# A fused attention and MoE kernel: the last chunk's second layer in seven block products instead of eight

## The chip, the cores and the metric

The kernel runs on one core of one Trainium2 chip. The metric is the device time of one execution in microseconds (us). Five engines work side by side, each on its own queue of instructions in a fixed order: PE (TensorE, matrix products into PSUM), DVE (VectorE), ACT (ScalarE), POOL (GpSimd) and SP (SyncE, which here issues the DMAs). PEld is TensorE's loading of weights, which overlaps its products.

## The reference

```
attn_out = softmax(q k^T / 8 + decay, causal) v      # 8 batches, 8 heads, 576 positions, 64 per head
x = attn_out as 4608 tokens x 512
h = x @ w_in                                         # 512 x 2048
g = h * tanh(softplus(h))                            # Mish
out = g @ w_out                                      # 2048 x 512
```

All arrays are float32.

## The kernel before, in words

Attention runs over 32 pairs of heads (8 batches of 4 pairs). The MoE part works on 9 chunks of 512 tokens: chunks 0 to 7 are the first 512 positions of the eight batches, chunk 8 (the last) gathers the 64 last positions of each of them. A float32 matrix is held as two float16 parts, hi and lo, and a product is made of three TensorE products (hi hi, hi lo, lo hi). The 2048 hidden columns are 16 blocks of 128 (`NF`).

**First layer.** For one block `j` and one chunk, `m1_items` issues 4 x 3 = 12 products of 128 x 512 into one PSUM bank, ScalarE applies Mish (tile `me`), and `halves` scales and splits the result into `gh` and `gl`. In the chunks 7 and 8 the blocks are taken in pairs (`TWINS`), and `m1_seven` makes a pair's 2 x 2 block product by seven products of half the width instead of eight (the scheme of Strassen and Winograd): 7 x 2 x 3 = 42 products of 128 x 256 in place of 24 of 128 x 512. It needs sums of the tokens' blocks (`sums_of`) and sums of the weights' blocks (`diffs_of`), made by VectorE and ScalarE, and VectorE combines the seven results (`tt` on PSUM and an SBUF tile). Seven pairs are so done; the blocks 12 and 15 stay single.

**Second layer.** `m2_items` issues 4 x 3 products of 128 x 512 for one block into the four PSUM banks 4 to 7, which collect all 16 blocks of a chunk; then ScalarE copies each bank to `ot` and a DMA of 256 KB stores it. The first layer has the banks 0 to 3. In chunks 7 and 8 four blocks of the first layer and four of the second take turns (`GJ`).

**What sets the order.** The kernel's code records operations, it does not issue them. `Program` lists them with what they read and write, and a planner (`forward`, `backward`, `schedule`) simulates the five queues with costs of its own, ten times over, and writes out the order that came out best; where an operation may run on ScalarE or VectorE (`nc.choose`), it picks one. So an edit in the last chunk can move instructions anywhere in the program. All recorded operations carry the source line of one helper (L332 before, L335 now), so the groups of the trace are told apart by their tiles. `me` is a ring of five tiles (`NME`), `wall` holds all weights, `xa` the chunks' tokens.

Of the kernel before, what the change touches and what calls it, by code (L numbers as in the profile page):

```python
# [682 lines left out]
def attn_moe(ctx: ExitStack, tc: tile.TileContext, qk, v, f, w_in, w_out, out):  # L683
# [222 lines left out]
    def scale_weights(t0, t1):  # L906

        m, c, t, v = (a[:, t0:t1].rearrange("p t x -> p (t x)") for a in (wsq, wsc, wiv, wba))
        nc.vector.tensor_scalar(out=c, in0=m, scalar1=2.0**-120, scalar2=None, op0=ALU.max)
        twins = [a for a, b in TWINS if t0 <= a and b < t1]  # L910
        if twins:
            a, b = twins[0], twins[-1] + 2
            one, two = (wsq[:, a + k : b : 2, 0].unsqueeze(2).to_broadcast([P, len(twins), 2]) for k in range(2))
            nc.vector.scalar_tensor_tensor(
                out=wsc[:, a:b, 0].rearrange("p (t k) -> p t k", k=2), in0=one, scalar=2.0**-120, in1=two,
                op0=ALU.max, op1=ALU.add)
# [43 lines left out]

    def gated(c, js):
        nc.vector.scalar_tensor_tensor(
            out=gsc[c][:, js], in0=wsc[:, js, 0], scalar=csx[c], in1=fac[min(c, 1)][:, js],
            op0=ALU.mult, op1=ALU.mult)

    def level_all():
# [3 lines left out]
        level2(1, slice(0, NF), r)  # L970

    def split_weights(i):
        x, j = worder[i]
# [54 lines left out]
    def scale_chunk3(c, i):  # L1028
        cosc[c] = col()
        nc.vector.scalar_tensor_tensor(  # L1030
            out=cosc[c], in0=cix[c], scalar=1.0 / GSH, in1=top[:, i : i + 1], op0=ALU.mult, op1=ALU.mult)


    st = {g: {} for g in range(B * NP)}
# [109 lines left out]

    more_e = cp.tile([P, NEX, CH], F32, name="more_e")
    late = cp.tile([P, 704], F32, name="late")
    def mm(o, l, r, start, stop):
        nc.tensor.matmul(out=o, lhsT=l, rhs=r, start=start, stop=stop)

# [447 lines left out]
    def flat16(t):  # L1597
        return (t if len(t.shape) == 2 else t.rearrange("p j t s -> p (j t s)")).bitcast(F16)

    def sums_of(c):  # L1600
        t = xa[c % 2] if c < B else xat
        if c < B:
            halves = [flat16(xa[1 - c % 2])[:, 2048 * d : 2048 * d + 2048] for d in range(2)]
            homes = [(x[:, 0:1024], x[:, 1024:2048]) for x in halves]
        else:
            v = sp.tiles["v32"]
            homes = [[v[2 * d + k].bitcast(F16)[:, 0:1024] for k in range(2)] for d in range(2)]
        spare = [x[:, 0:CH] for x in sp.tiles["pt"] + sp.tiles["x32"]]
        for d in range(2):
            ga, gb, f1, f2 = spare[4 * d : 4 * d + 4]  # L1610
            hi, lo = homes[d]
            sums[c, d] = [x.rearrange("p (k n) -> p k n", k=4) for x in (hi, lo)]
            for g, dt in ((ga, d), (gb, d + 2)):
                nc.choose(*([(e, "tensor_tensor", (), dict(out=g, in0=t[:, dt, 0], in1=t[:, dt, 1], op=ALU.add))]
                    for e in ("vector", "gpsimd")))
            n1, n2 = slice(0, 256), slice(256, CH)
            tt = nc.vector.tensor_tensor
            tt(out=f1[:, n1], in0=ga[:, n2], in1=ga[:, n1], op=ALU.subtract)
            tt(out=f1[:, n2], in0=gb[:, n2], in1=ga[:, n2], op=ALU.subtract)
            tt(out=f2[:, n1], in0=f1[:, n2], in1=ga[:, n1], op=ALU.add)  # L1620
            tt(out=f2[:, n2], in0=gb[:, n1], in1=f2[:, n1], op=ALU.subtract)
            split(hi, lo, (f1, f2))

    def split(hi, lo, fs):
        for k, f in enumerate(fs):
            w = slice(CH * k, CH * k + CH)
            nc.choose(*(scaled(hi[:, w], f, None, e) for e in ("scalar", "vector")))
            nc.choose(*(sub(lo[:, w], f, hi[:, w], e) for e in ("vector", "gpsimd")))

    def diffs_of(a):  # L1630
        k = [x for x, _ in TWINS].index(a)
        home = flat16((sp.tiles["qk32"] + sp.tiles["hl"] + ST2 + ST1 + [rk2])[k])
        hi, lo = home[:, 0:1024], home[:, 1024:2048]
        w1, w2 = (wall[:, place[0, j]] for j in (a, twin_of[a]))
        fa, fb = (more_e[:, k] for k in range(2))
        s1, s2 = (x[:, 0:CH] for x in sp.tiles["v32"][4:6])
# [10 lines left out]
        split(hi, lo, (s1, s2))  # L1647

    nseven = [0]

    def m1_seven(c, a):
        j = twin_of[a]

        def both():
# [27 lines left out]
            p1 = sp.tiles["hb"][k % 2][:, n1]  # L1682
            tt = nc.vector.tensor_tensor

            def mish(o, i_, i):
# [23 lines left out]
    def m2_items(c, j):  # L1709
        n = min(CH, NT - c * CH)  # L1710

        def dts(k):
            gh, gl = gt[c, j]
            nc.closing = nc.closing or len(nc.ops)

            ends = [b - 1 for a, b in groups] if c == 0 else [NF - 1]
            if j in ends and k == 0:
                scale_chunk3(c, NG_ if c else ends.index(j))
            for dt in range(k * MQ, (k + 1) * MQ):
# [148 lines left out]
    def w0(fn):  # L1868
        M.append((fn, 0))
# [3 lines left out]
    for c in range(NCHUNK):  # L1873
        cstart[c] = len(M)
        if c == 1:
            w0(level_all)
        if c:
            w0(lambda c=c: scale_chunk2(c))
        if c == B:
            for b in range(B):  # L1880
                w0(lambda b=b: scale_tails(b))
        if c == 0:
            done = i = 0
            while done < NF:
                if i < NF:
                    M.extend(m1_items(c, i))
                n = 0
                while i - done >= LAG0 and n < 2 and done < NF:
                    M.extend(m2_items(c, done))
                    done += 1  # L1890
                    n += 1
                    if i - done < LAG:
                        break
                i += 1
            continue
        pairs_of = [a for a, _ in TWINS if c >= C7 and (a >= PLAIN or c > C7)]
        later = {b for a, b in TWINS if a in pairs_of}
        if pairs_of:
            w0(lambda c=c: sums_of(c))
        for j0 in range(0, NF, GJ):  # L1900
            phases += 1
            if c == C7:
                for a in pairs_of:
                    if j0 <= a < j0 + GJ:
                        w0(lambda a=a: diffs_of(a))
            if c == C7 + 1:
                for a, _ in TWINS:
                    if j0 <= a < j0 + GJ and a not in done7:
# [4 lines left out]
            phases += 1  # L1913
            for j in range(j0, j0 + GJ):
                M.extend(x + (phases,) for x in m2_items(c, j))
        if c == C7:
            done7 = pairs_of

    ai = 0

    def run_a(upto):
# [104 lines left out]
```

## Time and profile before

| | |
|---|---|
| median of 3 runs | 1014.02 us (1012.45 to 1014.3) |
| the profiled execution, its own time | 1017.58 us |
| its span on the engines | 1015.8 us |
| PE busy | 975.0 us, 96% of the span |
| DVE busy | 731.1 us, 72% |
| ACT busy | 710.1 us, 70% |
| POOL busy | 19.3 us, 2% |

The span runs from the first instruction to the last write; what the own time has beyond it (1.8 us) is start and end. A busy share is a mean over stages with different limits, so a stage is read by itself, and the chain of waits says which engine ended a stage.

### The profile page before, as it was taken

The numbers are of one execution on the slowest core, as the hardware profiler recorded it, in microseconds if no ns is written. First come the engines' busy times: TensorE is split into PE (matmuls) and PEld (weight loads), VectorE is DVE, ScalarE is ACT, GpSimd is POOL, SyncE is SP. The second block draws the span as 40 slices with busy tenths as digits, with TensorE's granted clock in tenths as the row PEclk, the third lists the DMA queues.
The fourth block names the chain that finished last, engine by engine and source line by source line (L and its number), as shares of the span: only waits on it lengthen the run. The fifth ranks groups of instructions, "written<-read, shape, count | busy, mean of one in ns | idle before, by whom it ended". The sixth has DMA issues, their size and how long they took to land.

```text
span 1015.8 us, 20884 instructions
## 1 busy us (share of the span) xinstructions
PE 975.0 (96%) x7847; PEld 545.8 (54%) x7847; DVE 731.1 (72%) x2013; ACT 710.1 (70%) x1369; POOL 19.3 (2%) x80
## 2 busy tenths in 40 slices
PE   6899699989999999999999999999999999999998
PEld 5686344544555455555555554454554556656664
DVE  7999799997677676667677667676666669953432
ACT  3569799987777877777778777888787765434323
POOL 5000000000000000000000000000000000000000
PEclk8899899999999999999999999999999999999999
DMA  7878967588777766676667686776566542001001
GB/s 209 335 251 210 182 159 157 115 178 192 137 143 163 168 136 147 147 176 138 151 145 184 144 158 139 178 136 134 127 111 143 92 74 63 4 1 42 1 1 42
DMA packets 265079, 137.50 MB, mean 135 GB/s; under 512 B 237522, under 2 KB 237714, under 8 KB 264978
## 3 DMA queue, kind: packets, MB, share of 16 engines
q1 hardware_dynamic: 264978, 136.17, 59.3%
q8 instruction: 61, 1.00, 0.4%
q14 instruction: 40, 0.33, 0.1%
HBM read 45.46 MB, written 9.66 MB: 54 GB/s over the span
## 4 chain that ended last, share of the span: by engine, by line
PE 66%; DVE 16%; ACT 7%; DMA 6%; issue 3%; SPq 1%; POOL 0%; DVEq 0%; ACTq 0%
PE b L332 66%; DVE wall L332 3%; DVE b L332 2%; DMA pt<-hb 2%; DVE hb L332 2%; DMA qk<-in_qk_dram 1%; ACT junk L332 1%; DMA st<-hl 1%; ACT L332 1%; DVE xp L332 1%; ACT hb L332 1%; DVE vv L332 1%; DVE x L332 1%; DVE gl L332 1%; ACT more_e L332 1%
## 5 line engine op out<-in xcount | busy, mean ns | idle before, releaser
L332 PEld LDWEIGHTS <-wall 128*128 128x128 f16 x3372 | 323.1, 98 | 345.7 <-issue 12.1
L332 PE MATMUL b<-gh,wall 128*128 128x512 f16 x1152 | 367.1, 379 | 1.5 <-DVE gh L332 1.5
L332 PE MATMUL b<-xa,wall 128*128 128x512 f16 (+1 forms) x1602 | 345.5, 365 | 6.2 <-ACT me L332 2.2
L332 PE MATMUL b<-gl,wall 128*128 128x512 f16 x576 | 218.1, 379 | 0.4 <-DVE gl L332 0.4
L332 DVE SCALAR_TENSOR_TENSOR gl<-me,gsc,gh 128x512 f16<-128x512 f32 x144 | 106.5, 746 | 52.0 <-ACT gh L332 51.0
L332 ACT ACTIVATE me<-b,cinv 128x512 f32<-128x512 f32 (+1 forms) x130 | 85.0, 660 | 53.1 <-PE b L332 52.2
L332 PE MATMUL b<-st 67*64 67x64 f16 (+11 forms) x672 | 105.3, 299 | 7.6 <-DVE x L332 3.0
L332 DVE CUSTOM_DVE_ANT_0 b<-b,mskw 128x512 f32<-128x512 f32 (+2 forms) x168 | 94.2, 563 | 21.1 <-PE b L332 19.8
L332 PE MATMUL b<-vv,pt 128*128 128x65 f16 (+3 forms) x2464 | 96.0, 199 | 7.3 <-DMA pt<-hb 6.0
L332 PEld LDWEIGHTS <-st 67*128 67x128 f16 (+3 forms) x864 | 67.7, 101 | 54.6 <-issue 13.1
L332 PEld LDWEIGHTS <-pt 128*128 128x128 f16 (+1 forms) x2352 | 78.4, 103 | 32.2 <-DMA pt<-hb 8.4
L332 ACT ACT_TABLE_LOAD x70 | 89.8, 1283 | 2.7 <-DVE x L332 1.5
L332 ACT ACTIVATE rk<-b,mn 128x512 f32<-128x512 f32 (+3 forms) x126 | 63.8, 541 | 39.7 <-DVE mn L332 32.7
L332 ACT ACTIVATE more_e<-b,mn 128x512 f32<-128x512 f32 (+3 forms) x126 | 64.0, 542 | 32.6 <-DVE mn L332 29.3
L332 DVE TENSOR_TENSOR hb<-rk,hb 128x512 f16<-128x512 f32 x84 | 57.7, 686 | 26.2 <-ACT hb L332 26.0
L332 DVE TENSOR_TENSOR hb<-more_e,hb 128x512 f16<-128x512 f32 x84 | 57.7, 687 | 24.7 <-ACT hb L332 24.3
L332 ACT ACTIVATE gh<-me,gsc 128x512 f16<-128x512 f32 x82 | 59.0, 720 | 2.5 <-DVE gsc L332 0.5
L332 ACT ACTIVATE hb<-more_e 128x512 f16<-128x512 f32 x84 | 52.6, 627 | 5.9 <-DMA pt<-hb 5.3
L332 ACT ACTIVATE hb<-rk 128x512 f16<-128x512 f32 x84 | 52.6, 627 | 3.0 <-DMA pt<-hb 2.5
L332 DVE TENSOR_SCALAR gh<-me,gsc 128x512 f16<-128x512 f32 x62 | 29.8, 483 | 31.8 <-ACT me L332 30.6
L332 DVE TENSOR_TENSOR me<-b,hb 128x256 f32<-128x256 f32 x42 | 17.4, 420 | 48.7 <-PE b L332 48.2
L332 DVE SCALAR_TENSOR_TENSOR hl<-qk,qt,hl 128x576 f16<-128x576 f32 x56 | 44.2, 811 | 0.5 <-DMA st<-hl 0.5
(187 smaller groups left out, 1048.8 us busy)
## 6 DMA issues: line engine op xcount, KB each, us to landing
st<-hl SPq DMA_DIRECT2D x168, 144.0 KB
qk<-in_qk_dram SPq DMA_DIRECT2D x30, 576.0 KB
out_dram<-ot SPq DMA_DIRECT2D x36, 256.0 KB
v<-in_v_dram SPq DMA_DIRECT2D x30, 288.0 KB
wall<-in_w_in_dram SPq DMA_DIRECT2D x16, 512.0 KB
wall<-in_w_out_dram SPq DMA_DIRECT2D x16, 512.0 KB
pt<-hb SPq DMA_TRANSPOSE x168
vv<-in_v_dram SPq DMA_DIRECT2D x2, 288.0 KB
```

What stands on the lines that cost most here:

```text
L332: r = getattr(real[eng], method)(*a, **kw)
```

## The change

The last chunk's second layer is made by seven block products as well. A pair of blocks of the hidden layer (two blocks of 128) meets the output's four blocks of 128: the 512 x 256 part of `w_out` and the pair's 256 x 512 activations make two such 2 x 2 block products (the index `e`), of seven products each, each of three 128 x 256 products on TensorE. So a pair costs 42 products of 128 x 256 in place of 24 of 128 x 512. `diffs2_of` makes the sums of blocks of `w_out` (once for each pair); `operands`, called at the end of `m1_seven` in the last chunk, makes the sums of the activations' blocks and splits four operands in place of the two of `halves`; `m2_seven` issues the products for a group of four pairs (`KG`), step after step, and VectorE or ScalarE adds each step's result to accumulators in SBUF (`accs`, in the tiles `xp0`, `hb` and `ot`), which eight DMAs of 128 KB store. All 16 blocks now form pairs, so blocks 12 and 15 go into pairs in the first layer of chunks 7 and 8 too. `scale_weights` no longer gives a pair one common scale; `ratio` corrects for it in `operands`. The preparation moves: `sums_of` and `scale_tails` of the last chunk into chunk 7, `diffs_of` of one pair into chunk 6, one `diffs_of` and one `diffs2_of` into chunk 4 (with `me` tiles as scratch), seven `diffs2_of` into chunk 7.

```diff
-TWINS = [(0, 1), (2, 3), (4, 5), (6, 7), (8, 9), (10, 11), (13, 14)]
+TWINS = [(2 * i, 2 * i + 1) for i in range(NF // 2)]
+C2 = 7
+KG = (4,4,)
+CE = 4
...
+    def diffs2_of(k):
...
+        fa, fb, s1, s2 = scratch(n == 0)
+        for i, f in enumerate((fa, fb)):
+            w = wall[:, place[1, 2 * k + i]]
+            nc.choose(*([(e, "tensor_tensor", (), dict(out=f, in0=w[:, 0:512], in1=w[:, 512:1024], op=ALU.add))]
+                for e in ("vector", "gpsimd")))
+        n1, n2 = slice(0, 256), slice(256, CH)
+        tt = nc.vector.tensor_tensor
+        tt(out=s1[:, n1], in0=fa[:, n2], in1=fb[:, n2], op=ALU.add)
+        tt(out=s1[:, n2], in0=s1[:, n1], in1=fa[:, n1], op=ALU.subtract)
+        tt(out=s2[:, n1], in0=fa[:, n1], in1=fa[:, n2], op=ALU.subtract)
+        tt(out=s2[:, n2], in0=fb[:, n1], in1=s1[:, n2], op=ALU.subtract)
+        split(hi, lo, (s1, s2))
...
+    def operands(c, a, u1, u2):
...
+        nc.vector.tensor_tensor(out=t12[:, n1], in0=u1[:, n2], in1=u1[:, n1], op=ALU.subtract)
+
+        def less(o, x, y):
+            nc.vector.scalar_tensor_tensor(out=o, in0=x, scalar=r, in1=y, op0=ALU.mult, op1=ALU.subtract)
+
+        less(t34[:, n1], u2[:, n2], u1[:, n2])
+        less(t12[:, n2], u2[:, n2], t12[:, n1])
+        less(t34[:, n2], u2[:, n1], t12[:, n2])
...
+        for (hi, lo), x, s in zip(res, (u1[:, n1], t12, t34, u2), (f, f, f, fj)):
...
+            nc.choose(*(scaled(hi, x, s, e) for e in GHW))
+            nc.choose(*(scaled_rest(lo, x, s, hi, e) for e in GLW))
+        ops2[c, k] = res
+
+    def m2_seven(c, ks, first, last):
...
+        def step(w, begins, a, b, to):
+            for e in range(2):
+                o = bank_of(e, w)
+                for n, k in enumerate(ks):
+                    for m, (h, l) in enumerate(((0, 0), (0, 1), (1, 0))):
+                        nc.tensor.matmul(
+                            out=o, lhsT=a(k, e, h), rhs=b(k, l), start=begins and n + m == 0,
+                            stop=n == len(ks) - 1 and m == 2, skip_group_check=not begins)
+                for q in to:
+                    x = accs[c][2 * (e + q // 2 * 2) + q % 2]
+                    if (e, q) not in done and first:
+                        done.add((e, q))
+                        nc.choose(*(scaled(x, o, cosc[c], g) for g in ("scalar", "vector")))
+                    else:
+                        nc.vector.scalar_tensor_tensor(
+                            out=x, in0=o, scalar=cosc[c], in1=x, op0=ALU.mult, op1=ALU.add)
...
+        steps = [
+            (0, True, weight(0, 0), value(0, None), (1, 2, 3)),
+            (1, True, diff(1), value(1, 1), (1,)),
+            (0, False, weight(1, 0), value(3, 0), (0,)),
+            (2, True, diff(0), value(1, 0), (3,)),
+            (1, False, diff(2), value(2, 0), (3,)),
+            (1, False, weight(1, 1), value(2, 1), (2,)),
+            (2, False, diff(3), value(3, 1), (1,))]
...
+            if c > C7:
+                operands(c, a, u1, u2)
+                return
             for i, u in ((a, u1), (j, u2)):
                 halves(c, i, u, CH)
...
         if c == B:
-            for b in range(B):
-                w0(lambda b=b: scale_tails(b))
+            for a, _ in TWINS:
+                M.extend(m1_seven(c, a))
+            k = 0
+            for i, n in enumerate(KG):
+                M.extend(m2_seven(c, range(k, k + n), i == 0, i == len(KG) - 1))
+                k += n
+            continue
...
+        def ahead_of_last(j0):
+            if j0 == 0:
+                w0(lambda: scale_chunk2(B))
+                for b in range(B):
+                    w0(lambda b=b: scale_tails(b))
+                w0(lambda: sums_of(B))
+            for k in ((5, 6, 7), (), (), range(4))[j0 // GJ]:
+                w0(lambda k=k: diffs2_of(k))
+        if c == C7 - 1:
+            w0(lambda: diffs_of(NF - 4))
+        if c == CE:
+            w0(lambda: diffs_of(NF - 2))
+            w0(lambda: diffs2_of(4))
```

Three places of the written order. First, VectorE's queue at the end of the last chunk's first layer. Before, it ends with the last pair's combinations (into `me` from a bank `b`) and the `lo` parts `gl`:

```order
L332 TENSOR_TENSOR me_1_162<-b0_0_125,hb_1_153 128x256
L332 SCALAR_TENSOR_TENSOR gl_0_161<-me_0_159,gsc3_102,gh_0_160 128x512
L332 TENSOR_TENSOR me_2_165<-b0_0_125,hb_1_153 128x256
L332 TENSOR_TENSOR me_2_165<-b1_0_118,me_2_165 128x256
L332 TENSOR_TENSOR me_2_165<-b0_0_125,hb_1_153 128x256
L332 TENSOR_TENSOR me_1_162<-b1_0_118,me_1_162 128x256
L332 TENSOR_SCALAR gh_2_166<-me_2_165,gsc3_102 128x512
L332 SCALAR_TENSOR_TENSOR gl_2_167<-me_2_165,gsc3_102,gh_2_166 128x512
L332 SCALAR_TENSOR_TENSOR gl_1_164<-me_1_162,gsc3_102,gh_1_163 128x512
```

Now, for a pair in the middle of that chunk, the same queue holds the operands' sums (in `more_e`, with `late` as the column `ratio`), four `lo` parts (in `wall` and `qk32`), and an accumulation from bank 4 into `ot`, between the combinations of the next pairs:

```order
L335 SCALAR_TENSOR_TENSOR more_e_104<-me_1_162,late_105,more_e_104 128x256
L335 TENSOR_TENSOR me_3_171<-b3_0_121,hb_0_152 128x256
L335 SCALAR_TENSOR_TENSOR wall_69<-me_0_159,gsc3_102,wall_69 128x256
L335 TENSOR_TENSOR me_3_171<-b0_0_125,me_3_171 128x256
L335 SCALAR_TENSOR_TENSOR more_e_104<-me_1_162,late_105,more_e_104 128x256
L335 TENSOR_TENSOR me_4_174<-b2_0_120,hb_0_152 128x256
L335 SCALAR_TENSOR_TENSOR wall_69<-more_e_104,gsc3_102,wall_69 128x2x256
L335 SCALAR_TENSOR_TENSOR qk32_0_108<-me_1_162,gsc3_102,qk32_0_108 128x512
L335 TENSOR_TENSOR me_3_171<-b3_0_121,hb_0_152 128x256
L335 SCALAR_TENSOR_TENSOR wall_69<-more_e_104,gsc3_102,wall_69 128x2x256
L335 SCALAR_TENSOR_TENSOR ot_0_191<-b4_0_122,cols_93,ot_0_191 128x256
```

What a pair asks of VectorE has more than doubled, and combinations, on which TensorE's banks 0 to 3 wait, stand behind it in one queue.

Second, TensorE's queue where the last chunk's first layer ends. Before, the last single block's products (bank 3) are followed by the last group of the second layer, in products of 512:

```order
L332 MATMUL b3_0_121<-xa2_91,wall_69 128x512
L332 LDWEIGHTS wall_69
L332 MATMUL b4_0_122<-gh_0_160,wall_69 128x512
L332 LDWEIGHTS wall_69
L332 MATMUL b5_0_123<-gh_0_160,wall_69 128x512
L332 LDWEIGHTS wall_69
L332 MATMUL b5_0_123<-gl_0_161,wall_69 128x512
```

Now the last pair's last product (bank 3) is followed by the second layer's first group in products of 256 (the weights' sums stand in `xa`):

```order
L335 MATMUL b3_0_121<-xa2_91,wall_69 128x256
L335 LDWEIGHTS late_105
L335 MATMUL b3_0_121<-xa2_91,late_105 128x256
L335 LDWEIGHTS xa1_90
L335 MATMUL b7_0_107<-gh_1_163,xa1_90 128x256
L335 LDWEIGHTS xa1_90
L335 MATMUL b7_0_107<-gl_1_164,xa1_90 128x256
```

At this point 117 of the second layer's 336 products are already issued, spread between the pairs of the first layer; 219 follow.

Third, VectorE's queue at the start of chunk 7, ahead of and around that chunk's first two combinations. Before, weights' sums stand there (tiles `v32`, `more_e`):

```order
L332 TENSOR_TENSOR me_3_171<-b1_0_118,hb_0_152 128x256
L332 TENSOR_TENSOR me_0_159<-b0_0_125,hb_1_153 128x256
L332 TENSOR_TENSOR me_3_171<-b2_0_120,me_3_171 128x256
L332 TENSOR_TENSOR more_e_104<-wall_69 128x512
L332 TENSOR_TENSOR me_3_171<-b1_0_118,hb_0_152 128x256
L332 TENSOR_TENSOR v32_4_137<-more_e_104 128x256 x2
```

Now the last chunk's sums (`pt` from `xa2`, into `v32`) stand ahead of the first two combinations:

```order
L335 TENSOR_TENSOR pt_4_133<-xa2_91 128x512
L335 TENSOR_TENSOR pt_3_131<-pt_2_130,pt_0_128 128x256
L335 TENSOR_TENSOR xa0_89<-x32_0_140,xa0_89 128x512
L335 TENSOR_TENSOR v32_3_136<-pt_2_130,v32_2_135 128x512
L335 TENSOR_TENSOR pt_3_131<-pt_1_129,pt_3_131 128x256
L335 TENSOR_TENSOR me_4_174<-b1_0_118,hb_0_152 128x256
L335 TENSOR_TENSOR me_1_162<-b0_0_125,hb_0_152 128x256
L335 TENSOR_TENSOR pt_5_134<-xa2_91 128x512
```

Half of those sums came ahead of chunk 7's combinations, and the weights' sums of its third pair went behind them. Outside these places TensorE's queue also differs in its order from about a tenth of its length to a third of it, and again from its middle on.

## Rows read from the trace of the kernel before

**Rows 1.** The page: span, engines' busy time, TensorE's weight loads (count, busy, mean ns).
```profile
span 1015.8 us, 20884 instructions
PE 975.0 (96%) x7847; PEld 545.8 (54%) x7847; DVE 731.1 (72%) x2013; ACT 710.1 (70%) x1369; POOL 19.3 (2%) x80
...
L332 PEld LDWEIGHTS <-wall 128*128 128x128 f16 x3372 | 323.1, 98 | 345.7 <-issue 12.1
```

**Rows 2.** The chain of waits from 780 us on: start, us, what.
```profile
779.90 64.73 PE b L332 x545
...
863.58 148.54 PE b L332 x936
...
1012.19 0.69 ACT ot L332
```

**Rows 3.** Stretches: length; busy PE, PEld, DVE, ACT, POOL; clock granted; DMA share; GB/s.
```profile
0.00:60.00 60.00, 46.63 (x603) 37.98 (x603) 52.40 (x135) 30.93 (x73) 14.62 (x51) 0.89 0.76 254
60.00:130.00 70.00, 60.23 (x624) 41.89 (x623) 62.80 (x191) 55.38 (x112) 1.18 (x4) 0.95 0.86 214
```

**Rows 4.** The same view, from the end of chunk 6 to the last product.
```profile
836.00:856.00 20.00, 20.00 (x176) 11.36 (x175) 19.61 (x46) 12.04 (x24) 0.00 (x0) 1.00 0.28 66
856.00:866.00 10.00, 9.46 (x85) 8.05 (x84) 10.00 (x25) 6.34 (x12) 0.00 (x0) 1.00 0.15 54
866.00:903.00 37.00, 37.00 (x240) 23.33 (x239) 34.13 (x75) 16.03 (x32) 0.00 (x0) 1.00 0.01 3
...
912.00:1012.20 100.20, 100.10 (x630) 61.44 (x628) 34.62 (x68) 32.05 (x56) 0.00 (x0) 1.00 0.05 17
```

**Rows 5.** Timeline of PE in the last chunk: start, us, operation, count.
```profile
953.41 1.47 PE L332 MATMUL b<-v,hl 128*128 128x256 f16 x12
954.72 0.82 PE L332 MATMUL b<-xa,wall 128*128 128x256 f16 x6
...
1000.07 2.11 PE L332 MATMUL b<-xa,wall 128*128 128x512 f16 x9
...
1002.01 0.59 PE L332 MATMUL b<-gh,wall 128*128 128x512 f16 x2
```

**Rows 6.** Timeline of VectorE in chunk 7 and at the end of the last chunk.
```profile
886.25 0.28 DVE L332 TENSOR_TENSOR xp<-x,xp 128x128 f16<-128x128 f32 x1
...
887.30 1.41 DVE L332 SCALAR_TENSOR_TENSOR gl<-me,gsc,gh 128x512 f16<-128x512 f32 x2
890.40 1.89 DVE L332 TENSOR_TENSOR pt<-xa 128x512 f32<-128x512 f16 x3 [1.69 <-ACT xa L332]
893.15 1.09 DVE L332 TENSOR_TENSOR pt<-pt,pt 128x256 f32<-128x256 f32 x3
...
1000.83 0.49 DVE L332 TENSOR_SCALAR gh<-me,gsc 128x512 f16<-128x512 f32 x1
1001.35 1.43 DVE L332 SCALAR_TENSOR_TENSOR gl<-me,gsc,gh 128x512 f16<-128x512 f32 x2
```

**Rows 7.** Groups of VectorE's instructions, shapes apart: busy us, mean ns, idle before.
```profile
L332 DVE SCALAR_TENSOR_TENSOR gl<-me,gsc,gh 128x512 f16<-128x512 f32 x144 | 106.5, 746 | 52.0 <-ACT gh L332 51.0
L332 DVE TENSOR_TENSOR me<-b,hb 128x256 f32<-128x256 f32 x42 | 17.4, 420 | 48.7 <-PE b L332 48.2 <-ACT hb L332 0.3
L332 DVE TENSOR_TENSOR more_e<-wall 128x512 f32<-128x512 f16 x14 | 9.3, 682 | 0.0
L332 DVE TENSOR_TENSOR pt<-pt,pt 128x256 f32<-128x256 f32 x8 | 3.2, 418 | 0.0
```

**Rows 8.** DMA from 1006 to 1016 us in 40 slices of 0.25 us: busy tenths, GB/s.
```profile
DMA  0000000000029967991000000039941997000000
GB/s 0 0 0 0 0 0 0 0 0 0 0 82 369 385 213 279 377 360 33 0 0 0 0 0 0 0 139 369 385 156 41 352 377 279 0 0 0 0 0 0
```

**Rows 9.** Who kept PE waiting up to 850 us: total us, times, longest.
```profile
PE b L332 <- DMA pt<-hb: 6.0, 4, 2.5
PE b L332 <- DMA qk<-in_qk_dram: 5.6, 1, 5.6
```

More of the change, by code (lines that the diff above doesn't have):

```diff
@@ L909, in scale_weights @@
         nc.vector.tensor_scalar(out=c, in0=m, scalar1=2.0**-120, scalar2=None, op0=ALU.max)
[L910 to L916, printed above, removed]
         sums = sum_rows(c, psum(RB))
@@ L1030, in scale_chunk3 @@
         nc.vector.scalar_tensor_tensor(
-            out=cosc[c], in0=cix[c], scalar=1.0 / GSH, in1=top[:, i : i + 1], op0=ALU.mult, op1=ALU.mult)
+            out=cosc[c], in0=cix[c], scalar=(2.0 if c >= C2 else 1.0) / GSH, in1=top[:, i : i + 1], op0=ALU.mult, op1=ALU.mult)
     st = {g: {} for g in range(B * NP)}
@@ L1146, in attn_moe @@
     late = cp.tile([P, 704], F32, name="late")
+    ratio = late[:, 600:608]
+    fac.append(late[:, 608:624])
     def mm(o, l, r, start, stop):
@@ L1647, in diffs_of @@
         split(hi, lo, (s1, s2))
+    diffs2, ops2, accs = {}, {}, {}
+    def diffs2_of(k):
+        n = (k + 4) % 8
+        if n == 0:
+            hi, lo = wall[:, 2 * NF], wall[:, 2 * NF + 1]
+        elif n < 4:
+            hi, lo = (x.bitcast(F16) for x in sp.tiles["pt"][2 * n - 2 : 2 * n])
+        else:
+            home = flat16(xa[n // 2 - 2])[:, 2048 * (n % 2) : 2048 * (n % 2) + 2048]
+            hi, lo = home[:, 0:1024], home[:, 1024:2048]
+        diffs2[k] = [x.rearrange("p (k n) -> p k n", k=4) for x in (hi, lo)]
+        fa, fb, s1, s2 = scratch(n == 0)
[10 more added lines that the diff above has]
+        split(hi, lo, (s1, s2))
@@ new lines, in places @@
+    def places():
+        r = flat16(rk2)
+        x = [(r[:, 0:512], r[:, 512:1024]), (r[:, 1024:1536], r[:, 1536:2048])]
+        x.append((evs.rearrange("p a n -> p (a n)").bitcast(F16), mskw.bitcast(F16)))
+        k = sp.count["gh"]
+        g = [tuple(sp.tiles[t][(k + i) % NGH].bitcast(F16) for t in ("gh", "gl")) for i in range(NGH)]
+        x = [tuple(t.rearrange("p (a n) -> p a n", a=2) for t in y) for y in x + g]
+        w = []
+        for i in range(4):
+            a, b = place[1, 4 * i], place[1, 4 * i + 2]
+            w.append(tuple(wall[:, a : b + 1 : b - a, 256 + 512 * h : 512 + 512 * h] for h in range(2)))
+        x = x[0:5] + w[2:4] + x[5:] + w[0:2]
+        for k in range(6):
+            h = flat16((sp.tiles["qk32"] + sp.tiles["hl"] + ST2 + ST1)[k])
+            for i in range(2):
+                x.append(tuple(
+                    h[:, 1024 * i + 512 * n : 1024 * i + 512 * n + 512].rearrange("p (a n) -> p a n", a=2)
+                    for n in range(2)))
+        return x
@@ new lines, in m2_seven, with begin, bank_of, weight @@
+    def m2_seven(c, ks, first, last):
+        n1, n2 = slice(0, 256), slice(256, CH)
+        def begin():
+            if first:
+                scale_chunk3(c, NG_)
+                accs[c] = [x[:, 256 * i : 256 * i + 256] for x in (
+                    sp.tiles["xp0"][0], sp.tiles["hb"][1], *sp.tiles["ot"]) for i in range(2)]
+        def bank_of(e, w):
+            return psum((4, 5, 6, 7, 4, 5)[2 * w + e])[:, n2 if w == 2 else n1]
+        def weight(i, half):
+            return lambda k, e, h: wall[:, place[1, 2 * k + i], 512 * h + 256 * half + P * e : 512 * h + 256 * half + P * e + P]
+        def diff(i):
+            return lambda k, e, h: diffs2[k][h][:, i, P * e : P * e + P]
+        def value(i, x):
+            return lambda k, h: ops2[c, k][i][h] if x is None else ops2[c, k][i][h][:, x]
+        fresh = set(range(4)) if first else set()
+        def step(w, begins, a, b, to):
[11 more added lines that the diff above has]
+                        nc.choose(*(scaled(x, o, cosc[c], g) for g in ("scalar", "vector")))
+                    else:
+                        nc.vector.scalar_tensor_tensor(
+                            out=x, in0=o, scalar=cosc[c], in1=x, op0=ALU.mult, op1=ALU.add)
+                    left[e, q] -= 1
+                    if last and not left[e, q]:
+                        y = c * CH + 256 * (q % 2)
+                        nc.sync.dma_start(out=out[e + q // 2 * 2, :, y : y + 256], in_=x)
+        done = set()
+        left = {(e, q): (1, 3, 2, 3)[q] for e in range(2) for q in range(4)}
+        steps = [
[6 more added lines that the diff above has]
+            (2, False, diff(3), value(3, 1), (1,))]
+        return [(begin, 0)] + [(lambda x=x: step(*x), 650 * len(ks)) for x in steps]
@@ L1903, in attn_moe @@
                 for a in pairs_of:
[L1904 to L1908, printed above, removed]
+                    if j0 <= a < j0 + GJ and a < NF - 4:
                         w0(lambda a=a: diffs_of(a))
```

48 lines of the change are left out of this document (38 added, 10 removed).

## The prediction

> **What bounds the kernel now.** I read the page first: TensorE is busy for 975.0 of 1015.8 us, and no other engine comes near it [rows 1]. A mean hides stages, so the chain of waits came next. From 780 us to the last product it runs over TensorE's own products, but for some 19 us of VectorE between its two long pieces, where chunk 7's sums are made [rows 2]. Then the busy time by stretches: over the last 100 us TensorE is busy for 100.10 of 100.20 us while VectorE works for 34.62 and ScalarE for 32.05 [rows 4]. So there a product less is time won, as long as the other engines keep up. In the first 130 us it is another matter: TensorE stands still for 13.4 of 60 and 9.8 of 70 us, 23.1 us in all [rows 3], and there an edit of the products buys nothing by itself.
>
> **What the change removes on TensorE.** The last chunk's second layer goes from 16 blocks x 12 = 192 products of 512 columns to 8 pairs x 42 = 336 of 256. In the first layer the blocks 12 and 15 become a pair in two chunks: 2 x 24 products of 512 become 2 x 42 of 256. Together 240 of 512 go and 420 of 256 come. Their prices are read from start to start in a run of them: twelve of 256 take 954.72 − 953.41 = 1.31 us, 0.1092 each; nine of 512 take 1002.01 − 1000.07 = 1.94 us, 0.2156 each [rows 5]. So −240 x 0.2156 = −51.7 and +420 x 0.1092 = +45.9, **−5.9 us** net. The 256s cost a little more than half, which eats 0.6 of the ideal 6.5. The weights in both runs are loaded anew for each product, so the price includes what loading doesn't hide.
>
> The TensorE page of the Trainium skill (TensorE: Matmul & The Clock Gate, section Back-to-back issue gap) speaks against the change. It says that in a real stream of weight loads and products the spacing is set by both, about 81 ns at 128 columns and 131 ns at 512. On a straight line between these, 256 columns would cost about 98 ns (an estimate from that page), and the sum would be −240 x 0.131 + 420 x 0.098 = +9.7 us. The rows above, 0.2156 and 0.1092, are such a stream, and they contradict it.
>
> **What it adds on VectorE.** Its instructions overlap: three of 256 elements whose recorded length is 0.418 take 1.09 us together, so one follows the other after 0.336; 512 elements follow after 0.604, the scaled difference `gl` of 512 after 0.665 [rows 6, 7]. One that needs its predecessor's result starts after the full length (0.52 us from `gh` to `gl`, where `gh` lasts 0.49) [rows 6]. The new form, a scaled difference of 256, is not in the trace; it lies between 0.336 and 0.665, and I take 0.395, the 512's step less the 0.27 by which the plain ones differ.
> - One `diffs_of` and eight `diffs2_of` are new, each 4 x 0.604 + 4 x 0.336 = 3.8 us, 34 us in all. Two of them stand in chunk 4 and one old one in chunk 6, where VectorE has slack: 72% over the span [rows 1]. Seven stand in chunk 7. From that chunk's first combination to the last chunk's first one the order has 81 of 256, 44 of 512, 16 `gl` and 7 small ones, 67 us. TensorE has 336 products of 256 and 224 of 512 there, 85 us. I cost it at nothing; the cover is those 18 us.
> - In the last chunk, from its first combination to its last, the order has 33 scaled differences of 256, 51 plain ones of 256, 19 `gl`-like ones, 2 of 512 and 6 small ones: 13.0 + 17.1 + 12.6 + 1.2 + 2.0 = **45.9 us**. TensorE meanwhile issues 336 − 12 products of the first layer and 117 of the second, 441 x 0.1092 = **48.2 us**. VectorE is filled to 95%. If every instruction held it for its full length (0.48, 0.42, 0.75, 0.68), it would be 55 us, 7 more than TensorE has.
>
> What such a filling costs stands in three stretches of the trace: with VectorE busy for 19.61 of 20, 10.00 of 10 and 34.13 of 37 us, TensorE loses 0, 0.54 and 0 us [rows 4], because products of the second layer stand between those of the first. They do so here as well. So the price lies between 0.4 us (0.54 of 67, over 48) and 7; I take **+1.0 us**, near the low end, as the three stretches have the same combinations under a like load. A combination queues behind up to three operand instructions there, and TensorE's banks 0 to 3 wait for it.
> - The last pair: after TensorE's last first-layer product it has 84 products (9.2 us) before the first that needs that pair's second operand. VectorE has 15 instructions (7 us) up to the end of the operands, with a Mish and a split on ScalarE between them. Nothing, if not behind by then.
> - The 36 additions into accumulators: eight go to ScalarE, 28 to VectorE at 0.395, 11 us, of which 19 stand in the last 219 products (23.9 us), where VectorE has nothing else. Nothing.
> - At chunk 7's start half of the last chunk's sums (8 instructions, 4 x 0.604 + 4 x 0.336 = 3.8 us) stand ahead of the first combinations, and as much of weights' sums went behind. Nothing; if they wait for the late transposes, up to 3.8 us.
>
> ScalarE has slack: over the last 100 us it is busy for 32 [rows 4], and two splits more a pair and eight additions are some 15 us on top. POOL has nothing new. SP's queue only has eight output DMAs for four at the end.
>
> **The tail.** Before, the last bank's copy takes 0.69 us on ScalarE [rows 2], and its 256 KB move in about 0.7 us [rows 8]. Now the last addition has 256 columns (0.42 to 0.48 us on VectorE) and 128 KB follow. **−0.5 us**, between −0.6 and 0.
>
> **Elsewhere** the new order shuffles the first third. I take nothing, either way; the bounds are what single waits there cost, up to 5.6 us for one DMA [rows 9].
>
> **Sum.** Against the profiled execution's own time: 1017.6 − 5.9 + 1.0 − 0.5 = 1012.2. It stood 3.6 us above the median, so the median should come to 1014.0 − 5.4 = **1008.6 us**.
>
> **Rivals.**
> - *VectorE becomes the bound in the last chunk.* For it: 95% filling, chains of dependent sums. Against: the three stretches. With the full lengths, +7 in place of +1: 1014.6, no change. Halfway, 1011.6. The VectorE page of the Trainium skill (VectorE: DVE Perf Modes, Terms) leans that way: its DRAIN entry has the next operation wait until the pipe is empty. Independent ones here start 0.336 apart at a length of 0.418, so the trace doesn't bear that out for them.
> - *The early waits grow* (slower). The planner rewrote the order from a tenth to a third of TensorE's queue, where it waits for transposes `pt` and for `qk` [rows 9]. From 7.4 us more idle time on, a third of the 23.1, it is slower by more than a measurement tells: at +9, 1017.6. For: nothing held the old order's waits where they were. Against: the operations there are the same, and no row favours a sign. The same mechanism with the other sign gives 1005.
> - *Chunk 7's start is late:* sums that wait for the last transposes, 3.8 us, 1012.4. Against: 5.6 us of VectorE's work stand between the tail's last split and the first sum that needs it, and before, the way from the one (886.25 + 0.28) to the other (890.40) took 3.9 us [rows 6].
> - *A part of the weight load shows in every product* (slower). A load lasts 0.098 us [rows 1]. The 420 products that come and the 240 that go leave 180 loads more; if each cost all of its length beside the prices above, that is +17.6 and 1026; from 0.041 us each on it is slower. The run of 256s at 0.1092 holds a load for each product, so hardly. The TensorE page of the Trainium skill named above has a rule of this kind, with its +9.7.
>
> **How the numbers follow.** A measurement of this kernel tells 0.2% (2 us) from no change: below 1012.0 is faster, above 1016.0 slower. The forecast has 0.62, with its own range from 1006 to 1011.5; VectorE as the bound 0.14 (0.03 of it still faster, 0.08 the same, 0.03 slower); the early waits worse 0.07 (0.05 slower, 0.02 the same) and better 0.08; chunk 7's start 0.07 (0.02 faster, 0.05 the same); the weight loads 0.02. So 0.75 faster, 0.15 the same, 0.10 slower. The range goes from 1004.0 to 1014.0: below lies a part of the early waits' better case, above the slower cases and half of VectorE's, together under 0.2.
>
> **What would show it.** In the trace after: 1008 products of 256 at 0.109 us from start to start; in the last chunk's first layer TensorE without waits for VectorE's `me` of more than some 2 us in sum, and VectorE busy for nine tenths; the last 219 products without a gap; the end 3 us or so after the last product; the first 130 us with some 23 us of idle TensorE. Wrong would be: gaps at bank 0 to 3's combinations, TensorE's clock off its upper level of 2.4 GHz in the last 100 us (the granted clock was 1.00 there [rows 4]), or early idle time moved by more than 3 us.

## The result, and the profile after

The changed kernel takes 1005.28 us (median of 4 runs, 1003.53 to 1005.89) beside 1013.24 us for the kernel before: a ratio of 0.9918, 95% interval 0.9900 to 0.9937, or 8.3 us less (6.4 to 10.1). It is faster, by less than 1%; the forecast was 1008.6 us with a range from 1004.0 to 1014.0. The profiled execution is the fastest of the four (1003.53 us), while that of before stood above its median, so the two spans (1001.7 and 1015.8 us) lie further apart than the kernels do.

The page after, the lines that answer to [rows 1]:

```profile
span 1001.7 us, 21440 instructions
PE 965.0 (96%) x8026; PEld 561.2 (56%) x8026; DVE 795.3 (79%) x2170; ACT 727.5 (73%) x1411; POOL 22.5 (2%) x79
...
L335 PEld LDWEIGHTS <-wall 128*128 128x128 f16 x3368 | 323.2, 98 | 322.0 <-issue 13.7
```

VectorE has 64 us more, TensorE 10 less, and TensorE still sets the time. The chain of waits from 780 us on has the same two long pieces as [rows 2], with VectorE between them:

```profile
790.80 59.66 PE b L335 x474
...
871.05 127.41 PE b L335 x1024
```

Now the stretches, columns as in [rows 3]: the start, then from the attention's last product to the last product of all (in three pieces), and the part of the last chunk from its first combination to its last:

```profile
0.00:60.00 60.00, 46.79 (x612) 38.05 (x612) 52.59 (x136) 31.73 (x76) 18.61 (x51) 0.97 0.79 268
60.00:130.00 70.00, 64.67 (x651) 43.13 (x648) 68.12 (x197) 60.13 (x126) 0.41 (x3) 1.00 0.83 209
...
828.99:903.00 74.01, 73.77 (x467) 45.44 (x466) 66.91 (x149) 34.41 (x63) 0.00 (x0) 1.00 0.06 19
903.00:976.00 73.00, 73.00 (x612) 59.67 (x610) 64.45 (x149) 44.24 (x84) 0.00 (x0) 1.00 0.04 16
976.00:998.48 22.48, 22.44 (x206) 19.87 (x203) 13.87 (x32) 1.98 (x3) 0.00 (x0) 1.00 0.11 37
927.00:975.50 48.50, 48.50 (x446) 43.39 (x445) 46.41 (x112) 34.23 (x66) 0.00 (x0) 1.00 0.04 15
```

In the last row VectorE is busy for 46.41 of 48.50 us and TensorE for all 48.50: VectorE is filled to 96% (the forecast: 45.9 of 48.2, 95%), and TensorE loses nothing by it. From the attention's last product to the last product of all it stands still for 0.24 us, in one wait for `st` in chunk 7; before, it was 0.54. (The 0.04 us in the third piece and the 0.10 in the last row of [rows 4] stand behind the last product, which ends at 998.44 and 1012.10.)

The timeline of TensorE gives the price of a product of 256: seventeen from 980.70 to 982.56, 0.109 each, as in [rows 5].

```profile
980.70 2.02 PE L335 MATMUL b<-wall 128*128 128x256 f16 x17
982.56 0.27 PE L335 MATMUL b<-gh,wall 128*128 128x256 f16 x1
```

VectorE's timeline of one pair shows the form that was not in the trace before, the scaled difference of 256 columns. It lasts 0.48 us, and the next instruction starts 0.39 to 0.40 after it (forecast: 0.395). The second row below does not need the first one's result:

```profile
945.77 0.48 DVE L335 SCALAR_TENSOR_TENSOR v<-me,late,me 128x256 f32<-128x256 f32 x1
946.17 0.48 DVE L335 SCALAR_TENSOR_TENSOR v<-me,late,v 128x256 f32<-128x256 f32 x1
946.56 0.48 DVE L335 SCALAR_TENSOR_TENSOR wall<-me,gsc,wall 128x256 f16<-128x256 f32 x1
946.96 0.48 DVE L335 SCALAR_TENSOR_TENSOR v<-me,late,v 128x256 f32<-128x256 f32 x1
...
997.17 0.48 DVE L335 SCALAR_TENSOR_TENSOR xp<-b,cols,xp 128x256 f32<-128x256 f32 x1 [0.83 <-PE b L335]
998.48 0.48 DVE L335 SCALAR_TENSOR_TENSOR hb<-b,cols,hb 128x256 f32<-128x256 f32 x1 [0.82 <-PE b L335]
```

The last row is the last addition. From there to the end are 3.3 us (3.6 before, from 1012.19 in [rows 2]). Who kept TensorE waiting up to 850 us, against [rows 9]: `pt` 2.4 us (6.0 before), `qk` 5.1 (5.6); the waits for ScalarE's `me` and `more_e` grew to 5.4 and 5.3 (2.2 and 1.6 before).

```profile
PE b L335 <- ACT me L335: 5.4, 5, 2.1
PE b L335 <- ACT more_e L335: 5.3, 5, 1.6
PE b L335 <- DMA qk<-in_qk_dram: 5.1, 1, 5.1
...
PE b L335 <- DMA pt<-hb: 2.4, 4, 0.8
```

**Where the time came from.** The attention's last three products (on `tv`) split the execution; every product that the change touches stands behind them. Before, then now:

```profile
844.35 0.27 PE L332 MATMUL b<-vv,tv 128*128 128x65 f16 x3
...
828.72 0.27 PE L335 MATMUL b<-vv,tv 128*128 128x65 f16 x3
```

The late part took 171.45 us before (844.35 to 1015.8) and 172.98 now (828.72 to 1001.7), 1.5 us more; the spans are printed to 0.1 us, so such times are good to 0.05. But the written order has other products in it: 474 of 512 and 588 of 256 columns before, 273 and 1008 now, by the forecast's prices 166.4 and 168.9 us, 2.5 more. Beyond the products the late part so gained 1.0 us, and with the products' own -5.9 the change is worth **-6.9 us** there. The rest of the -8.3, some 1.4, would be in the early part, whose order is new. But the interval of the -8.3 holds -6.9 too, so the times alone don't show it.

### The profile page after: what moved, and what is told of

Same layout as the page of the kernel before. It is cut to its first block, busy times and chain, and to the rows that moved or that the text cites. A ratio compares the mean times of both kernels' runs of the same rounds, so it can differ in the third digit from the quotient of the medians.

```text
span 1001.7 us, 21440 instructions
## 1 busy us (share of the span) xinstructions
PE 965.0 (96%) x8026; PEld 561.2 (56%) x8026; DVE 795.3 (79%) x2170; ACT 727.5 (73%) x1411; POOL 22.5 (2%) x79
## 4 chain that ended last, share of the span: by engine, by line
PE 60%; DVE 17%; ACT 8%; DMA 7%; issue 4%; SPq 3%; DVEq 0%; ACTq 0%
PE b L335 60%; DVE b L335 3%; SPq L335 3%; DMA st<-hl 3%; DMA pt<-hb 2%; DVE wall L335 2%; DVE hb L335 2%; DVE hl L335 1%; ACT hb L335 1%; DMA qk<-in_qk_dram 1%; DVE vv L335 1%; ACT rk L335 1%; ACT junk L335 1%; ACT x L335 1%; DVE gl L335 1%
## 5 line engine op out<-in xcount | busy, mean ns | idle before, releaser
L335 PE MATMUL b<-xa,wall 128*128 128x512 f16 (+1 forms) x1604 | 339.5, 362 | 7.5 <-ACT me L335 5.4
L335 PE MATMUL b<-gh,wall 128*128 128x512 f16 (+1 forms) x1068 | 337.1, 374 | 1.1 <-DVE wsc L335 1.0
L335 PE MATMUL b<-gl,wall 128*128 128x512 f16 (+1 forms) x534 | 199.9, 374 | 0.0
L335 DVE SCALAR_TENSOR_TENSOR gl<-me,gsc,gh 128x512 f16<-128x512 f32 x131 | 97.4, 747 | 37.2 <-ACT gh L335 36.6
L335 PE MATMUL b<-st 67*128 67x512 f16 (+11 forms) x672 | 105.3, 297 | 8.0 <-ACT more_e L335 4.7
L335 PEld LDWEIGHTS <-pt 128*128 128x128 f16 (+1 forms) x2424 | 83.0, 101 | 28.5 <-DMA pt<-hb 5.7
L335 PE MATMUL b<-vv,pt 128*128 128x65 f16 (+4 forms) x2464 | 93.5, 197 | 3.2 <-DMA pt<-hb 2.4
L335 PEld LDWEIGHTS <-st 128*128 128x128 f16 (+3 forms) x816 | 62.6, 101 | 52.7 <-issue 11.5
L335 ACT ACTIVATE gh<-me,gsc 128x512 f16<-128x512 f32 x75 | 53.5, 718 | 1.6
L335 DVE SCALAR_TENSOR_TENSOR wall<-wall 128x512 int32<-128x512 int32 x64 | 42.8, 687 | 0.1
```

Source lines behind the costliest of these rows:

```text
L335: r = getattr(real[eng], method)(*a, **kw)
```

## The experiments

Three theories after the result, with the numbers that e1 and e2 give them. Theory 1: the forecast's sum holds in the last two chunks, and the rest comes from the new order of the first third. Theory 2: all of it is in the last two chunks, and the forecast's sum there was too small. Theory 3: most of it is early. (The later runs number theories of their own.) And on VectorE: does its filling cost anything, and where does it begin to? Times of the late part below go from the start of the last `tv` products to the end, in each run's profile.

**The start's order** (e1, e2, e3 and e12). The order that the planner writes is cut at 300 us of its own time; ahead of the cut stands a list of operations from the other kernel's order, behind it the rest:

```diff
-        order = self.warmed(*self.schedule(deps))
+        order = pinned(self.warmed(*self.schedule(deps)))
...
+def pinned(order):
+    pre = np.frombuffer(zlib.decompress(base64.b85decode(PIN)), np.int32).tolist()
+    pre = [(x // 4, x % 4) if x >= 0 else (-1, 0) for x in pre]
+    seen = {i for i, _ in pre}
+    return pre + [x for k, x in enumerate(order) if (x[0] not in seen if x[0] >= 0 else k >= OWN)]
```

The changed kernel with the start of before (e1):

> The changed kernel, with the first 300 us (planned time) of all five queues in the order of the kernel before. Theory 1 (the forecast's sum holds in the last two chunks, about -5.2 us, and the rest of the -8.0 us, some 2.8, comes from the new order of the first third): 1008.1 us. Theory 2 (all of it comes from the last two chunks, the early order is worth nothing): 1005.3 us, as the change. Theory 3 (most of it is early, as the profiled pair shows, 6 us by the end of chunk 0): 1011 us, and the last chunks give only some 2.

1006.63 us (1003.21 to 1009.29), 0.9919 (0.9902 to 0.9937): -8.2 us (-9.9 to -6.4). This is theory 2's figure (1005.3 beside 1013.24 is 0.9922); theory 1's 1008.1, 0.9949, lies outside the interval. The late part is as in the changed kernel, 172.99 us.

The kernel before with the start of the changed one (e2):

> The kernel before, with the first 300 us of all queues in the order of the changed kernel (and so without the seven instructions that give a pair one common scale; each block has its own). Theory 1: 1010.4 us. Theory 2: 1013.2 us, as before. Theory 3: 1007 us. The early idle time of TensorE should then read as in the changed kernel (5 us and not 10 between 60 and 130 us) if the order makes it.

1011.47 us, 0.9971 (0.9959 to 0.9983): -2.9 us (-4.2 to -1.7), as theory 1 had it, where theory 2 had nothing. The late part is unmoved (171.32 us). The stretch from 60 to 130 us:

```profile
60.00:130.00 70.00, 66.52 (x651) 43.97 (x651) 67.54 (x195) 59.53 (x124) 0.42 (x3) 0.95 0.83 209
```

TensorE's idle time there is 3.5 us (9.8 in [rows 3]). Over all traces it is 3.5 to 5.9 us in the nine with the changed kernel's start and 7.5 to 9.8 in the four with that of before, so the order makes it and not the chance of one execution.

Behind the cut, e2 has what the planner writes without the common scale, and this differs from the order of before too, mostly between 500 and 800 us. Its gain still stands ahead of 300 us: from there to the last `tv` products TensorE is idle for 6.8 us in both, at a granted clock of 1.00 (before, then e2):

```profile
300.00:844.35 544.35, 537.57 (x4289) 278.46 (x4287) 374.66 (x1060) 412.02 (x788) 2.63 (x19) 1.00 0.67 141
...
300.00:837.88 537.88, 531.06 (x4260) 275.63 (x4258) 370.62 (x1047) 409.10 (x782) 2.63 (x19) 1.00 0.67 141
```

The two gains don't add up (-8.2 and -2.9 against -8.3 for both), but e1's interval is 3.5 us wide, and -6.9 with a start worth 1.7 to 2.9 fits within all of them. The traces say more than the times. The eight of the changed kernel with its own start (itself and e5 to e11) reach the last `tv` products at 827.58 to 830.75 us; e1, with the same order behind the cut, is 2 to 5 us later, though in one execution only:

```profile
832.71 0.27 PE L410 MATMUL b<-vv,tv 128*128 128x65 f16 x3
```

The kernel before without the common scale, in its own order (e3):

```diff
-        twins = [a for a, b in TWINS if t0 <= a and b < t1]
-        if twins:
...
-            nc.vector.scalar_tensor_tensor(
-                out=wsc[:, a:b, 0].rearrange("p (t k) -> p t k", k=2), in0=one, scalar=2.0**-120, in1=two,
-                op0=ALU.max, op1=ALU.add)
```

> The kernel before in its own order throughout, without the seven small VectorE instructions for a pair's common scale (each block has its own scale). Theory 1 and 2: nothing, 1013.2 us within 1. Rival: they stand in the chain that scales the weights, and TensorE waits for its end in the first 130 us; at 0.3 us each this is up to -2, 1011.2 us.

1014.91 us, 0.9999 (0.9987 to 1.0012): these seven instructions (0.155 us each in the trace of before) cost nothing themselves. As e2 and e3 hold the same instructions, what parts them is order alone. But with the seven gone the planner writes the changed kernel's start: over the first 300 us of its time the two orders differ by 0.3 places per operation in the mean, and from the order of before by 22. So this small part of the diff, not the last chunk, moved the start.

A third start, which the planner gives with fewer rounds (`FB = 4` in place of 9), ahead of the kernel before without the common scale (e12):

> The kernel before without the common scale, with a third order of all queues for the first 300 us (planned), which the same planner gives with five rounds in place of ten, and the later order that the planner gives without the common scale. Theory 1 (the order of the start is worth some us either way, and the changed kernel drew a better one): between 1008 and 1018 us, and not that of the run with the new start (ratio 0.9971) by more than its interval. Theory 2 (any order of the start costs the same, and the 2.9 us of that run came from what follows it): 0.9971 again.

1018.32 us, 1.0027 (1.0002 to 1.0052): +2.7 us (0.2 to 5.3), and not the -2.9 of e2. So theory 1 of this run: the order of the start is worth some us. That this one is slower than before is barely clear of noise. And not all of it need be in the start: the late part took 172.6 us, 1.3 more than in e2, which has the same written order there.

**The eighth pair alone** (e4), in the kernel before, whose order is kept for 500 us; the common scale is left out here too:

```diff
-TWINS = [(0, 1), (2, 3), (4, 5), (6, 7), (8, 9), (10, 11), (13, 14)]
+TWINS = [(2 * i, 2 * i + 1) for i in range(NF // 2)]
```

> The kernel before with its own order for 500 us, and the eighth pair (blocks 12 to 15 as two pairs) in the first layer of the last two chunks; second layer as before, no common scale. TensorE: -48 products of 512 at 0.2156 and +84 of 256 at 0.1092, -1.2 us: 1012.0 us if VectorE hides the one more sum of weights and the combinations; 1013.2 or more if a combination of the new pair makes TensorE wait.

1013.65 us, 0.9989 (0.9977 to 1.0001): -1.1 us (-2.3 to +0.1), which by the times alone is not clear of nothing; the late part is 170.40, 1.05 less than before. So most of its share of the products' term (-1.2) is there.

**The changed kernel again** (e5), unaltered:

> The changed kernel once more, unaltered, beside the other runs of its chip, for a closer ratio to before. If the late part gives -6.9 us (end of attention to the end in the profiled pair: TensorE's products -5.9, its gaps -0.35, the tail -0.4, the rest reading error) and the early order between 0 and -2.9, the ratio is 0.9904 to 0.9932: 1004.9 to 1007.8 at a before of 1014.7.

1004.54 us, 0.9913 (0.9887 to 0.9938), -8.8 us. As a ratio, beside a before of 1014.02 us, it lies in what was expected (0.9904 to 0.9932), and its interval holds both ends.

**VectorE's load in the last chunk.** Each operation of `less` in `operands` is issued `TIMES` times, in place:

```diff
-            for eng, method, a, kw in ops[i][0][o][1] if i >= 0 else self.warm[1]:
-                r = getattr(real[eng], method)(*a, **kw)
+            for _ in range(TIMES if i in self.extra else 1):
+                for eng, method, a, kw in ops[i][0][o][1] if i >= 0 else self.warm[1]:
+                    r = getattr(real[eng], method)(*a, **kw)
...
         def less(o, x, y):
+            nc.extra.add(len(nc.ops))
```

`TIMES = 0` (e6):

> The changed kernel without 24 of VectorE's instructions in the last chunk's first layer, three scaled differences of 256 columns for each of the eight pairs (so the operands and the output lack these sums); all else in the same order. VectorE has 24 x 0.395 = 9.5 us less in 73. Theory 1 (VectorE's filling costs TensorE nothing there, as the gaps of 0.04 us in the last chunk say): as the changed kernel within 0.5 us. Theory 2 (the forecast's +1.0 us for the filling): 1 us faster. Theory 3 (the combinations come late by what stands ahead of them, hidden as slower products): several us faster.

1005.43 us, 0.9911 (0.9890 to 0.9932), late part 173.02: theory 1. Taking 9.5 us off VectorE gives TensorE nothing, since it stood nowhere: it is busy for all of 75 us, as it was for all of 73 with them.

```profile
903.00:978.00 75.00, 75.00 (x623) 60.76 (x621) 58.26 (x129) 44.54 (x84) 0.00 (x0) 1.00 0.04 15
```

`TIMES = 2` (e7):

> The changed kernel with these 24 instructions each issued twice (the same result is written again), in place, all else in the same order: 9.5 us more for VectorE in the last chunk's first layer, where the trace has it busy for 64.5 of 73 us. Theory 1 (its idle 8.5 us take it in first, then TensorE waits): 0 to +2 us. Theory 2 (the forecast's sum by steps from start to start, 45.9 of 48.2 us: all above 48.2 is added): +7 us. Theory 3 (every added instruction delays the next combination): +9.5 us.

1016.76 us, 1.0017 (1.0002 to 1.0032); late part 183.04, **+10.1 us**, above all three theories and nearest to theory 3 (+9.5). TensorE now loses 7.0 of 75 us, waiting for the operands and the combinations:

```profile
903.00:978.00 75.00, 68.00 (x548) 53.37 (x547) 65.97 (x151) 40.01 (x76) 0.00 (x0) 1.00 0.04 15
```

```profile
PE b L338 <- DVE wall L338: 2.6, 3, 0.9
PE b L338 <- ACT hb L338: 2.0, 1, 2.0
PE b L338 <- DVE xp L338: 1.4, 1, 1.4
PE b L338 <- DVE me L338: 1.3, 3, 0.5
PE b L338 <- DVE gl L338: 1.0, 1, 1.0
```

`TIMES = 4` (e8):

> The same with each of the 24 issued four times: 72 more, 28.4 us at 0.395. All theories have VectorE as the bound by now. Theory 1: +20 us (28.4 less the idle 8.5). Theory 2: +26. Theory 3: +28. If the form takes its recorded length of 0.48 or so each instead of 0.395, some 6 us more in each.

1045.10 us, 1.0306 (1.0283 to 1.0329), late part 213.65, +40.7 us. All three expectations were too low for e8, with the 6 us more too (28 + 6). Its VectorE timeline shows a price they all had wrong:

```profile
936.29 2.04 DVE L338 SCALAR_TENSOR_TENSOR v<-me,late,me 128x256 f32<-128x256 f32 x4
938.25 2.04 DVE L338 SCALAR_TENSOR_TENSOR v<-me,late,v 128x256 f32<-128x256 f32 x4
```

Four copies take 2.04 us, so a copy starts (2.04 - 0.48)/3 = 0.52 after the one before, which writes the same place; the next row starts 1.96 after the first. With 0.52 for a copy, e7 adds 24 x 0.52 = 12.5 us, and with the 2.1 us that VectorE had left (48.50 less 46.41) the late part should grow by 10.4; it grew by 10.1. (The 0.52 and the 2.1 were read after these results, so e7 and e8 don't test them.) For e8 it is 37.4 - 2.1 = 35.3 and measured 40.7; the rest goes with the clock granted to TensorE, which stood at 0.91 and 0.89 once TensorE waited much:

```profile
903.00:960.00 57.00, 50.07 (x350) 35.93 (x349) 46.45 (x104) 22.61 (x41) 0.00 (x0) 0.91 0.05 20
960.00:1010.00 50.00, 36.55 (x280) 29.38 (x279) 45.22 (x101) 20.30 (x39) 0.00 (x0) 0.89 0.00 1
```

That the clock makes all of the difference wasn't tested apart. Eight copies only (e9; `nc.extra.add` at the first `less` of each pair, `TIMES = 2`):

> The changed kernel with one of the three scaled differences of each pair issued twice: 8 instructions more on VectorE in the last chunk's first layer. From the 24 more, which cost 9.8 us from the end of attention to the end (182.8 against 173.0 us), at 0.48 us each (11.5 us): the changed kernel has some 1.7 us of room left there. Theory 1 (such a room): 3.8 less 1.7, +2 us. Theory 2 (each added instruction is on the path, 0.41 each): +3.3 us. Theory 3 (room for a third of them, and only the queue behind many is slow): 0.

By 0.52 it is 4.2 - 2.1 = +2.1. The late part is 175.72, **+2.7 us**, between theory 1 (+2) and theory 2 (+3.3), with 1.79 us of new gaps (71.21 of 73):

```profile
903.00:976.00 73.00, 71.21 (x592) 57.70 (x591) 65.70 (x152) 43.02 (x81) 0.00 (x0) 1.00 0.04 16
```

The times alone, 1006.37 us and 0.9913 (0.9895 to 0.9931), don't tell it from the changed kernel: 2 us is what a measurement here can tell.

**The second layer's groups**, with the changed kernel's order up to the last chunk. One group of eight pairs (e10, `KG = (8,)`):

> The changed kernel, in its own order for 850 us (planned), with the last chunk's second layer in one group of eight pairs: the same 336 products, 18 additions less on VectorE and ScalarE, but 49 products of the second layer instead of 117 between the first layer's. Theory 1 (those products are the cover for VectorE's work): 68 x 0.108 = 7.3 us less cover, some 3 us less work in that phase, 1.7 of room: +2 to +3 us. Theory 2 (VectorE's total counts, not the cover): 0, or some faster by the additions that went.

1006.14 us, 0.9904 (0.9885 to 0.9923); late part 173.99, +1.0 us, 0.75 of it gaps (96.25 of 97 us from 903 to 1000). Less than theory 1's +2 to +3. From the last chunk's first combination to its last TensorE loses nothing, with VectorE filled to 98%; the new gaps stand behind that stretch, at 972.12 and 973.53, where products wait for operands (`qk`, `hl`):

```profile
926.76:968.98 42.22, 42.22 (x384) 37.36 (x383) 41.41 (x99) 29.56 (x57) 0.00 (x0) 1.00 0.07 26
```

Why more than half of the cover could go at so little cost wasn't tested. It is not the additions that went: in the changed kernel only 5 of them stood on VectorE in that stretch. Four groups of two (e11, `KG = (2, 2, 2, 2)`):

> The changed kernel, in its own order for 850 us (planned), with the last chunk's second layer in four groups of two pairs: the same products, 36 additions more, 120 products of the second layer between the first layer's (117 before). Theory 1 (cover as before, room of 1.7 us, about half of the additions fall into the first layer's phase, 18 x 0.48 = 8.6): +7 us. Theory 2 (additions are hidden in the second half, where VectorE has slack): 0 to +2 us.

1007.93 us, 0.9923 (0.9907 to 0.9939); late part 175.74, +2.8 us, of which 2.0 stand in one row of the waits, for additions into `ot`:

```profile
PE b L517 <- DVE ot L517: 2.0, 2, 1.5
```

Closer to theory 2 (0 to +2) than to theory 1 (+7). In the trace VectorE makes 65 additions (28 in the changed kernel), and 17 of them (5) end before the last combination; the other 25 more fall where it has slack. The 12 more are 4.7 us by their steps where 2.1 were left, so +2.6, and VectorE is now full there:

```profile
926.70:978.98 52.28, 50.75 (x459) 44.68 (x457) 52.10 (x126) 35.57 (x67) 0.00 (x0) 1.00 0.06 21
```

These are instructions of another kind than the copies, so this run bears the account out. No version beat the changed kernel by what can be told.

## Why the prediction was right, and where its terms were off

**The products (-5.9 us): right.** 0.109 us a product of 256 holds in the new streams, and the eighth pair by itself gave -1.05 in the late part where its share is -1.2. The rule of the Trainium skill (TensorE: Matmul & The Clock Gate, Back-to-back issue gap) puts 512 columns in a stream of loads and products at about 131 ns, and +9.7 us was worked out from it. It isn't borne out by this stream, with 215.6 ns for 512 columns and 109 for 256.

**VectorE's filling (+1.0 us): the amount of work was right, its price was not.** The work was put at 45.9 of 48.2 us; 46.41 of 48.50 was measured. The step that failed is the one that took a loss from the stretch where TensorE stood still for 0.54 of 10 us and carried it over. Nothing is lost here (0 of 48.50 us), nothing comes back when VectorE has 9.5 us less to do (e6), and from the point where its 2.1 us of room are used up nearly every us is on the path (from e9 to e7 8.3 us more work, 7.4 us more time). In these runs it is an edge, not a slope; where it lies is known to 1 us (4.2 - 2.7 = 1.5 us of room by e9, 12.5 - 10.1 = 2.4 by e7). So the rival in which VectorE becomes the bound did not come true, but 8 instructions more begin it (e9), and at full lengths (55 us) it would have. The instructions go by their steps: 0.39 to 0.40 for one that lasts 0.48. The DRAIN entry of the Trainium skill (VectorE: DVE Perf Modes, Terms) says that the next operation can't issue until the pipe is empty. The traces bear that out only where an instruction needs its predecessor's result (0.52 us from `gh` to `gl` in [rows 6]) or writes the same place (copies 0.52 apart at a length of 0.48).

**The tail (-0.5 us): right,** 3.3 us from the last product's end to the end in place of 3.7, -0.4.

**Elsewhere (nothing): the other term that was off.** The prediction named this part, put it at 0 and gave a better start 0.08. (In the traces TensorE's order differs from its seventh product on, and not only from a tenth of its queue.) Its own sign for being wrong, early idle time moved by more than 3 us, came: from 23.1 to 13.2 + 5.3 = 18.5 us. The new start gives -2.9 us (-4.2 to -1.7) in the kernel before, and the late part's -6.9 leaves 1.4 for it in the changed one. Which of the two it is there stays open, since the times of the runs with and without it (e5 and e1, 0.9913 and 0.9919) can't be told apart; in its one trace e1 is 2 to 5 us behind where the early part ends, which speaks for the larger. The price of a new start could not be read from rows, but its spread could have been allowed: the two new starts that were run gave -2.9 and +2.7 (0.2 to 5.3).

With -6.9 for the late part and -1.4 for the start the sum is -8.3, where the -1.4 is only what is left over; the forecast had -5.4. Both terms that were off erred the same way, and 1005.28 lies below the range of the forecast's own case (1006 to 1011.5). That the whole range held it is owed to the room left for a better start, and so in part to luck. Chunk 7's start, the weight loads and the early waits growing (the other rivals) left no trace: TensorE stands still for 0.24 us in all of the late part, and less than before in the first 130 us.

## What to carry to other kernels

An engine filled to 96% beside the one that bounds can cost nothing; here products that don't wait for it stood between, but how many of them it takes was not found (e10). Count its instructions at their start-to-start steps, compare with the bounding engine's time over the same stretch, and expect the loss to begin where the two are about equal. Where a planner rewrites the order, deleting seven small instructions that cost nothing themselves can move the time by some us through the start's order; give it a spread of its own, and test it by grafting one kernel's start on the other, with the order behind the graft kept too. When executions scatter by as much as the effect, measure the stretch between two fixed events in the traces beside the whole time.

## What was not expected of the hardware

The clock granted to TensorE in the first 130 us differs from order to order, and from execution to execution of one order. The stretch from 60 to 130 us in the third start (e12) and in the changed kernel's second run (e5):

```profile
60.00:130.00 70.00, 64.45 (x643) 45.28 (x642) 69.35 (x195) 56.35 (x128) 0.73 (x3) 0.93 0.83 226
```

```profile
60.00:130.00 70.00, 64.14 (x633) 42.63 (x626) 67.96 (x196) 60.07 (x123) 0.41 (x3) 1.00 0.82 206
```

TensorE is as busy in both, but was granted 0.93 and 1.00. In e2, which has the changed kernel's start, it was 0.95. The twelve runs of e12 range from 1010.8 us (mean granted clock over the span 0.990) to 1025.1 (0.980); the ten of the changed kernel from 1003.1 to 1008.2 (0.992 to 0.998). The clock is not all of it, as the slowest of those ten had 0.997. So a start is judged by the clock that it is granted too, and not by TensorE's busy time alone.
